# A fused attention and maxout kernel whose order table is planned anew with longer DMA steps

## The chip, the cores and the metric

The kernel runs on one core of a Trainium2 chip. The metric is device time in microseconds for one execution. Five engines work side by side, each through its own instructions in order: TensorE (PE in the profile; its weight loads are PEld), VectorE (DVE), ScalarE (ACT), GpSimd (POOL) and SyncE (SP), which here issues nearly all DMAs.

## The reference

Two layers follow each other. The first is attention with a threshold: only scores within `tau` of the row's maximum take part. The second is a feed-forward layer whose hidden value is the maximum of three products.

```
scores = q @ k.T / sqrt(64)                  # 8 batches, 8 heads, 576 rows
keep   = scores >= max(scores) - tau         # tau = 0.02
attn   = softmax(where(keep, scores, -1e9))
x      = attn @ v                            # laid out as 4608 x 512
h      = max(x @ w1, x @ w2, x @ w3)         # 4608 x 768
out    = h @ w_out                           # 4608 x 512
```

## The kernel before, in words

**The work.** A quad is four heads of one batch; there are 16. Its q and k are loaded (`qm`, `km`), transposed on PE (tile `tp`) and evacuated to `qt` and `kt`, by ACT or by DVE; POOL (in the first quad DVE too) makes `qs`, a copy of `qt` with its halves swapped. A quad has nine chunks of 128 rows by 2 x 576 scores, 144 in all; in batches 0 and 7 the nine are done in two parts, four and five.

**One half chunk** of 128 x 576 scores (tile `sc`, 288 of them) passes so: PE multiplies (letter `S`); DVE takes the row maximum (`m`), writing the negated scores to `z`; ACT makes the exponents in one or two passes (`e`, `n`); the sums lead to a reciprocal on DVE (`r`); POOL normalises into the bf16 tile `P` (`p`). A DMA transpose issued by SP turns a whole chunk (`t`, tile `ptq`); when a quad's chunks are there, PE multiplies them by v (`O` and `D`, tile `o`; a product), and the result is copied to `xt` (`x`, `w`).

**The feed-forward layer** follows batch by batch in pieces of two halves (`F` and `B`): hidden pieces (tile `ph`, from `xt` and the weights `w`), whose maximum is built by `h`, `H` and `v` in `hm` and `hT`, and output pieces (tile `po`), copied to `ob` by `u` or `U` and stored by `o`. The weights arrive in twelve loads (`g`) through borrowed tiles and are cast to bf16 by POOL, DVE or ACT (`z`, `b`, `f`).

**What sets the order.** `ORDER` is a text with one letter per step; the loop at the kernel's end walks through it, so the text fixes the order on every engine. A digit behind `S`, `T`, `F`, `N` or `O` names the PSUM bank, of which there are four, each large enough for one such tile. The case of some letters picks the engine: `A`, `c` evacuate on DVE, `a`, `C` on ACT; a threshold for the exponent is worked out on DVE by `s`, on POOL by `d`. `TILES` gives the order of the chunks within a quad's part. `MASKED` has one digit for each half chunk: 0 goes over `z`, with a threshold and two ACT passes; 1 has one ACT pass, and DVE removes what is below the threshold (`k`); 2 and 3 are as 0 and 1, but ACT reads the scores from PSUM directly, and 2 needs no threshold. In a direct half chunk the bank stays taken until ACT has read it.

The three tables were written by a planner that is not part of the file.

Of the kernel before, what the change touches and what calls it, by code (L numbers as in the profile page):

```python
# [35 lines left out]


# [10 lines left out]
ORDER = """
lllllllllllT1lT0lagqqcT3T2aS1CqqgS3mgS0emS2yynmeS1emgmT3eS0AeT2kgS3nqmT1CqAnT2rklS1eqmCS0nqmepS2eprrmS3emS1p
tmnS0pS3smnkpteeS2prmnzmtemepekpeS2lS0ylrbyS1nnlmtpnpmnrremptebS3peS0mnS1mS2znrpmS0eptmmnlpS3pemdlreekS0S1ms  # L50
kT3nAnO20lpeerwdDgpxtmnnT3S0eprectpmS2mtS3nprqS0mT1epAptT3S1plqenmbnO20CdrmpDlkxewzS3eegmlS0pF2mksBrF3HtS1Bd
S2nntqmeteepvlnF0BS1mqS3egvzRnppmT2nS0pmAndmrpS1peempeS2S1mgknpmegtretF3BkHS0tmS2pmetS1npS3mT2rsneF0zmsnyBcr
S1enpsvnO32S0peemDpwsmpwS1nF3S0smrzBrqS1nstmF2vBsT3S0ppemHenteAS1psF2mlT3zyBqrgcvsnS3F0nemgS2plpelnmepS3mtyB
ellqrmetqvnpS2sprdmO13fpsS0nDweS1mtewzkmnerS2S0F3dsnpS1mBpmeteepkF2mdtT0BnlulllneRnF1kAstS3pBHnmvF0epyRS2Btm
ppeS1S3vqtnmdS2F0pS1lpmneT3edCmpBF2emslnlT3aT1kHdqeBctRvS0ypF3S1ptnpmnmrdpBF2qS0S1vmenBmtedS3S0HepmnrqF1T2Bm
pseanS3velF2T0sT1CapkmBS0etvetS1rS3ppmmkmS0npnO21eetS3seDxrpmpnmqS0kytS3smpkxS2rmettpdS1emF0pesS3mmrS2nelBS1
nkmeqlduT3pmlpS2skeemCnO10kRsDwwldtS3pS1pmmtepeeF0S2qspdS3BmnmF1F2eneBBqhrkrF0S3pvpsBvT2S1snempndeapHterpllm
S3eF0mnS2dmS1myBqF3rF2nptS1vlsBsnBT0rmvpeS1ppnhncmS3mF2enntsrtF0BByevpF3rS1vemnppS2mF0eydBtS1thF2kBdBeS3tqmr
vevnlpO01S2DpnlmexkesemT2pwadF3eplS0kdT1tmBCqRHeS2dmpS0onS1nF3lmS2nmBelynnF0F1tpdtmqspBBevvphS3S2rS0nsseemF1
reF3ppmBntpBmrsdS0pveevS2nmmS1F3mlpertpT0BAypkepqS1UmnkF2tS0edS3entornS1mmBmtpeeueS3nS1ptkksrmmpO20ltnsrpDlk  # L60
S1rpS3mmxS2epxepT0mqcdnN1eT3AkdnBF2S0jS3meT1deBeqqcRF0S1pHBS2mtF3mBdnppS1monennpvdlrstS2vF0meeF3mBnherBkpevS
2lF1T0mappkslT3BrtvCnS2F0mpqS3S1detS2enBptmlmshpS3eS1prdmppmneF0lrlS2dF3ntBmmseBevsS2F1tpT0psBtrvymnAtS3hS2p
demnmO01S2kwenenpDS3ermT0nrwF2qlmtspncqpqrS1pedBF3mplevetS0plBS1mdeF2S0vpndBmmdorkhF3S1T2tBmS0eepS1ndatvdmtF
3pktndmRF2S0plemnpBdvBF1HS0mS3enpmrpnBeF2eT0CdqevBnlS3S1vepS0S2qptmmenmtkrsF3nS0edT1pmtlAemBT2srS1puqeS0pncm
nO32mekrtDweS0weqS1F2F3psmnpmnkplsS0eRkyepmByS1ekBmpsS0ypundmF2hS1RptemplBS0ndF3vdpmlT1BS2AdnmpevlF0S1BF2S3n
rlmBF1emdeehF0kpeBvnS3veemBsF2S1hrtS0ntplqBlnpF3mmnT1vBqsRtkyS0pF2tteCevS1omppBnS3S0hF2ptldpndmmBsenmS3pT1ye
aensvmeRS0etmpolS2skO31pDemT0wqwF2S3ctpdemBqF1ieS0T3pBvmS2tF0ndndaeF3hkymRdBqnvBF2pevsepS1lT0tBmpCrHpeS3ntS1
mS0nmdF2F3mBBS0perntnpevvpsnS1S2F3ltmrdepmepS0mBS2sT1kdmelUnF0tdS3nnpqmrS2ApnpT1BsemtS3RemnlN2CpS1kesBsppeer
qUlmeS0mmS3T1jT2tS0mdnasceltpO13menslqDypS0wknrxpS1mpmlyF3dT2BldS0eAspntHnnrS1pmtF2merpF3BqeBsS0vnenrvyF1S2B
enpS3mS0spptpmmmsS2heeF1rS3BpS0mF2nmF3mvteeBqtBF0eT1vHnkBF2S3dnsBrCnpF1vdemlS0BevqpykeF3mS2hrBprnmvF0eqtndts  # L70
S1prmleBO32nspDpvpeF1S0nwekS3wsBmnepdtS2hmF0T1mdpBS2AF3vS1erBF0etndmS2nmrnpeS1vBnF3mpsnT2ylpRpdCoeHmBpS0dS2e
vS1emmF3T0mBvS2asetpnnS0telpepqmmntrS1F3tpS2S0BmskeodmprtlknF1UeprmpqS2sT3eptcpmqsnBS0tS2mekudnS3O01Dkerpnmx
lexqrmpslS2dmpS3S1tF0mpleennermlS2BddF3mHnS1tpBrT0F2snmAS1eBevF0vpnptnqS3BmdlterHemtF2nslpS1tmBF0T3BpvsdCvyr
F1nedeS3rpltpeF2T0meBBS3tAHvmpF0F1qtqBpS2vnBS3pF0mS2mneBkerkhelO13tqnesmevsxklrpDS2nS1xF0T3pBmtmF1eCepkdS3S2
vBnrmpS0eS3phtmT2nF1mT0amnkpdBrqersvF3pS2BCF1S0mnT2BsevF3ompdrepqpS0thAmBdvS1peF2mtS0npBnmvS3S1S0deqrmpF2imT
3nBnptsreCpmqS3UmnseS0ekmtrodeF1petS2tmkepeBS3kO02psmtrDwN3ndpuexerpS0meF1S2BeF0mBBnjF2hnS1kyskvdeptBS0mmrF3
ptvdpS1nrpmBF0S2BnHnvF1epF3mBF0rveBBS2lykhF3vepS1mBnF0ddmS2F1venBS3mRtdHepmBnvS2depmS0oF3F1ptBmeBS0vehS3tnpn
knperlmsF2pF1mssBprvBppF3S0tvmeekBhnrteF2tS1F0BpmvsBenedS1nvmkrS3mpS2F0S1npetemrBmypeS2tO31umyspnDwwepO20xDe
skerpkS1pmF2S3oS1snrntextprpBpmnmF3F1BF0epUBnhprtBkdepF3F2ttvnprBtpBvhvF1pF3tBvBHoF0F2BBO13vDxvO20wDF3wwF1F2
F0oBHUuF1BBF2F3BhvoF0BvBiF1vF2BvF3BhvBvF2F1ouN0Bujooi  # L80
"""


# [728 lines left out]
```

## Time and profile before

| | |
|---|---|
| median of 3 runs | 441.38 us (440.68 to 441.64) |
| profiled execution, its own time | 440.52 us |
| its span | 438.7 us |
| PE busy | 418.6 us (95%) |
| DVE busy | 396.3 us (90%) |
| ACT busy | 393.7 us (90%) |
| POOL busy | 324.4 us (74%) |
| DMA transposes, median to landing | 144, 4.3 us |

The profiled execution lies 0.86 us under the median; sums are made against 440.52 us and carried over to the median. Every instruction of the kernel passes through one recording helper, so all rows of the profile name line 100, and groups are told apart by tile names (`z<-sc` writes `z` and reads `sc`). A PE matmul with fp32 operands stands as two matmuls in the profile. From step 72 on, two half chunks in eleven use the tile `stage` in place of `z`.

### The profile page before, as it was taken

How to read it: one execution, taken by the hardware profiler on the slowest of the kernel's cores; microseconds unless marked ns; L12 is line 12 of the kernel's file. 1: busy time of each engine (PE TensorE's matmuls, PEld its weight loads, DVE VectorE, ACT ScalarE, POOL GpSimd, SP SyncE). 2: the span in 40 equal slices, each digit the busy share in tenths (PEclk: the TensorE clock that was granted, in tenths of full speed). 3: DMA queues.
4: the chain of work that ended last, by engine and by line, in shares of the span. 5: the costliest groups of instructions: out<-in, count | busy, mean ns of one | idle time of the engine just before them, and what ended most of it. 6: DMA issues, size and time to landing. Idle time of an engine off the chain costs nothing.

```text
span 438.7 us, 14399 instructions
## 1 busy us (share of the span) xinstructions
PE 418.6 (95%) x5357; PEld 315.5 (72%) x5359; DVE 396.3 (90%) x1126; ACT 393.7 (90%) x813; POOL 324.4 (74%) x491
## 2 busy tenths in 40 slices
PE   8768889999999999999999999999999999999995
PEld 6455556775787877877787787877778777886962
DVE  3989999999999999999999999999999988998741
ACT  4999998999999999999999999999999999789412
POOL 3798999897689768878888868985887787467400
PEclk9969999999999999999999999999999999999999
DMA  9999999999998999999979997999998785788921
GB/s 264 317 232 228 205 265 249 246 202 224 232 199 177 261 211 226 164 234 201 211 157 213 267 220 153 167 233 191 233 198 156 182 192 83 155 149 155 206 87 73
DMA packets 211590, 87.98 MB, mean 201 GB/s; under 512 B 186944, under 2 KB 199744, under 8 KB 211520
## 3 DMA queue, kind: packets, MB, share of 16 engines
q1 hardware_dynamic: 210704, 86.40, 95.0%
q8 instruction: 42, 0.69, 0.7%
q10 hardware_dynamic: 816, 0.66, 0.5%
q14 instruction: 28, 0.23, 0.2%
HBM read 35.13 MB, written 9.44 MB: 102 GB/s over the span
## 4 chain that ended last, share of the span: by engine, by line
PE 76%; ACT 9%; DVE 6%; issue 3%; DMA 3%; POOL 1%; SPq 1%; DVEq 0%; POOLq 0%; ACTq 0%
PE ph L100 28%; PE sc L100 26%; PE po L100 10%; ACT z L100 8%; PE o L100 8%; PE tp L100 4%; DVE z L100 4%; DMA qm<-in_q_dram 2%; DMA ptq<-P 1%; DVE hm L100 1%; POOL P L100 1%; PE warm L100 1%; SPq L100 1%; DVE hT L100 0%; DVE kt L100 0%
## 5 line engine op out<-in xcount | busy, mean ns | idle before, releaser
L100 POOL TENSOR_SCALAR P<-z,rs 128x576 bf16<-128x576 f32 x250 | 193.3, 784 | 36.6 <-DVE rs L100 13.0
L100 DVE TENSOR_SCALAR_CACHE_REDUCE z<-sc 128x576 f32<-128x576 f32 x250 | 182.4, 750 | 9.9 <-PE sc L100 6.8
L100 PE MATMUL sc<-kt,qs 64*128 64x320 f32 (+2 forms) x640 | 181.5, 416 | 7.9 <-ACT z L100 5.0
L100 PE MATMUL sc<-kt,qt 64*128 64x256 f32 (+2 forms) x640 | 183.0, 427 | 0.9 <-ACT z L100 0.4
L100 PE MATMUL ph<-xt,w 64*128 64x288 bf16 (+2 forms) x2304 | 174.0, 283 | 0.4
L100 PEld LDWEIGHTS <-w 64*128 64x128 bf16 x2304 | 128.4, 94 | 30.8 <-issue 3.0
L100 ACT ACTIVATE z<-z 128x576 f32<-128x576 f32 x186 | 125.5, 679 | 0.3
L100 ACT ACTIVATE z<-z,th 128x576 f32<-128x576 f32 x159 | 118.6, 767 | 1.6 <-DVE th L100 1.0
L100 PEld LDWEIGHTS sc<-kt,qs 64*128 64x128 f32 (+1 forms) x640 | 91.9, 178 | 24.7 <-ACT z L100 7.4
L100 PEld LDWEIGHTS sc<-kt,qt 64*128 64x128 f32 (+1 forms) x640 | 91.6, 178 | 15.1 <-DVE z L100 2.5
L100 POOL COPY qs<-qt 64x640 f32<-64x640 f32 (+1 forms) x62 | 44.3, 715 | 15.9 <-ACT qt L100 9.1
L100 PE MATMUL po<-wo,hT 64*128 64x512 bf16 (+2 forms) x454 | 54.4, 354 | 0.8 <-DVE hm L100 0.4
L100 DVE SCALAR_TENSOR_TENSOR z<-z 128x576 f32<-128x576 f32 x64 | 51.5, 807 | 0.1
L100 POOL TENSOR_SCALAR th<-nm 128x1 f32<-128x1 f32 x95 | 28.6, 301 | 28.1 <-DVE z L100 11.9
L100 PE MATMUL o<-ptq,vb 128*64 128x512 bf16 (+4 forms) x720 | 43.5, 276 | 1.2 <-DMA ptq<-P 0.7
L100 ACT ACTIVATE z<-z,nm 128x576 f32<-128x576 f32 x57 | 43.1, 768 | 0.0
L100 PEld LDWEIGHTS <-hT 64*128 64x128 bf16 (+1 forms) x456 | 31.1, 94 | 15.7 <-issue 2.4
L100 DVE TENSOR_TENSOR hm<-ph,hm 128x576 bf16<-128x576 f32 (+2 forms) x48 | 36.1, 752 | 5.6 <-PE ph L100 4.5
L100 PEld LDWEIGHTS <-vb 128*64 128x64 bf16 (+1 forms) x720 | 26.0, 109 | 20.9 <-issue 10.4
L100 DVE TENSOR_TENSOR hT<-ph,hm 128x576 bf16<-128x576 f32 (+2 forms) x48 | 36.2, 753 | 2.2 <-PE ph L100 0.6
L100 ACT ACTIVATION_READ_ACCUMULATOR z<-z 128x1 f32 x186 | 36.7, 198 | 0.0
L100 POOL TENSOR_SCALAR P<-stage,rs 128x576 bf16<-128x576 f32 x38 | 29.0, 768 | 5.0 <-issue 3.1
(55 smaller groups left out, 413.8 us busy)
## 6 DMA issues: line engine op xcount, KB each, us to landing
vm<-in_v_dram SPq DMA_DIRECT2D x32, 256.0 KB, 3.9
qm<-in_q_dram SPq DMA_DIRECT2D x15, 512.0 KB, 4.7
km<-in_k_dram SPq DMA_DIRECT2D x15, 512.0 KB, 5.5
out_dram<-ob SPq DMA_DIRECT2D x14, 512.0 KB, 3.7
ptq<-P SPq DMA_TRANSPOSE x144, 4.3
v<-in_v_dram SPq DMA_DIRECT2D x16, 96.0 KB, 3.1
hT<-in_moe_w_dram SPq DMA_DIRECT2D x3, 512.0 KB, 10.0
stage<-in_moe_w_out_dram SPq DMA_DIRECT2D x3, 512.0 KB, 5.9
```

The costliest lines, as they stand in the source:

```text
L100: ins = fn(*a, **kw)
```

## The change

The planner was run anew with every step of the DMA queue counted four per cent longer. The file differs in the three tables alone: the order of steps, the digits of `MASKED`, the order of chunks in `TILES`, and the banks and engines that the letters name. The number of scores, products, hidden pieces, transposes and loads is what it was. Counted over the whole text, these letters change: `s` 94 to 85 and `d` 95 to 107; `r` and `R` together 128 to 131 instructions; `k` 72 to 73 and `n` 216 to 215; evacuations of `tp` on DVE 31 to 28 and on ACT 33 to 36; weight casts on DVE 3 to 5, on ACT 1 to 0, on POOL 8 to 7; output copies on DVE 7 to 6, on ACT 11 to 12. The direct digits among the first 72 half chunks go from 32 to 28.

```
 MASKED = """
-233222232202322222212300021210200220321222000000000310000010020100001001
+233222232222322222232320003102000200000001000000100310000010020100001001
...
 TILES = """
-065106157238447283620314785243875061513472860765830421817650432357816042
+106560512834787243321604785243871506351472608035786412817065432581376042
...
 ORDER = """
-lllllllllllT1lT0lagqqcT3T2aS1CqqgS3mgS0emS2yynmeS1emgmT3eS0AeT2kgS3nqmT1CqAnT2rklS1eqmCS0nqmepS2eprrmS3emS1p
+llllT2llT3ACqT2lqT3aS0lqqClS3meS1S2mmS0neelmeyS3mlymT1lAllS2keT1necT0rmqqnaggS3qlT1qnmS0CS1eeS2mpkrmpS3gepS0
...
```

At the very start the rows on PE are the same up to the first scores, but the tiles behind them are not: `T1 T0 T3 T2` took four banks for the first four groups of transposes, `T2 T3 T2 T3` takes two. PE before (`tp` with a number is one bank's tile; `qm`, `km` are the loads, `q9`, `k9` their ninth columns):

```order
L100 MATMUL tp_136<-identf_58,qm_116 128x64 x8
L100 MATMUL tp_136<-identf_58,q9_121 128x64 x2
L100 MATMUL tp_148<-identf_58,km_117 128x64 x8
L100 MATMUL tp_148<-identf_58,k9_122 128x64 x2
L100 MATMUL tp_169<-identf_58 128x128 x8
L100 MATMUL tp_169<-identf_58,qm_116 128x64 x8
L100 MATMUL tp_186<-identf_58 128x128
L100 MATMUL tp_186<-identf_58,km_117 128x64 x8
L100 MATMUL sc_197<-kt_167,qs_161 128x256
L100 MATMUL sc_197<-kt_167,qt_160 128x320
```

PE now:

```order
L100 MATMUL tp_126<-identf_58,qm_116 128x64 x8
L100 MATMUL tp_126<-identf_58,q9_121 128x64 x2
L100 MATMUL tp_139<-identf_58,km_117 128x64 x8
L100 MATMUL tp_139<-identf_58,k9_122 128x64 x2
L100 MATMUL tp_156<-identf_58 128x128 x8
L100 MATMUL tp_156<-identf_58,qm_116 128x64 x8
L100 MATMUL tp_175<-identf_58 128x128
L100 MATMUL tp_175<-identf_58,km_117 128x64 x8
L100 MATMUL sc_186<-kt_153,qt_150 128x256
L100 MATMUL sc_186<-kt_153,qs_151 128x320
```

`tp_156` lies in the bank of `tp_126`, so it waits for the evacuation of that tile. That evacuation has moved from ACT to DVE. DVE before, at the same place:

```order
L100 COPY qs_161<-qt_160 64x2x320
L100 COPY kt_167<-tp_148 128x2x320
L100 COPY qs_161<-qt_160 64x2x256
L100 TENSOR_SCALAR z_208,nm_209<-sc_197 128x576
L100 TENSOR_SCALAR z_216,nm_217<-sc_205 128x576
```

DVE now:

```order
L100 TENSOR_SCALAR qt_150<-tp_126 128x2x320
L100 COPY qs_151<-qt_150 64x2x320
L100 COPY qs_151<-qt_150 64x2x256
L100 TENSOR_SCALAR z_197,nm_198<-sc_186 128x576
L100 TENSOR_SCALAR z_207,nm_208<-sc_194 128x576
```

DVE evacuates `qt` first, and the copy to `kt` has gone to ACT.

The second place is POOL about two thirds through the program, where thresholds (`th`) have come over from DVE. POOL before:

```order
L100 TENSOR_SCALAR P_5664<-z_5406,rs_5659 128x576
L100 COPY qs_5522<-qt_5521 64x2x320
L100 CAST vb_5726<-vm_5273 128x1024
L100 TENSOR_SCALAR P_5751<-z_5464,rs_5659 128x576
L100 TENSOR_SCALAR P_5751<-z_5473,rs_5659 128x576
L100 TENSOR_SCALAR P_5765<-z_5476,rs_5723 128x576
L100 TENSOR_SCALAR P_5765<-z_5515,rs_5723 128x576
L100 TENSOR_SCALAR P_5809<-z_5558,rs_5723 128x576
```

POOL now, from the same normalisation (the 194th) on:

```order
L100 TENSOR_SCALAR P_5676<-z_5413,rs_5652 128x576
L100 TENSOR_SCALAR P_5690<-z_5456,rs_5652 128x576
L100 TENSOR_SCALAR th_5750<-nm_5629 128x1
L100 TENSOR_SCALAR th_5766<-nm_5684 128x1
L100 TENSOR_SCALAR P_5690<-z_5496,rs_5652 128x576
L100 TENSOR_SCALAR P_5785<-z_5530,rs_5779 128x576
L100 TENSOR_SCALAR th_5798<-nm_5707 128x1
L100 TENSOR_SCALAR P_5785<-z_5536,rs_5779 128x576
```

Three thresholds now stand between normalisations where none stood; each waits for a row maximum of DVE, and the normalisations behind it wait with it.

More of the change, by code (lines that the diff above doesn't have):

```diff
@@ L24 @@
 MASKED = """
-233222232202322222212300021210200220321222000000000310000010020100001001
+233222232222322222232320003102000200000001000000100310000010020100001001
 011010100100100000000010001100000000000111102100100000101000000100001100
-000000101000110100010000100001000100000100000100000100000001100010000000
-000011010010000000000001011100100000001110001100001001000110000012100010
+000000101000110100000100000001000100000100000100100100000000110000010000
+000011012010100000011001000000001000001110111000100010000110000012100010
 """
 TILES = """
-065106157238447283620314785243875061513472860765830421817650432357816042
-762315804786502134175623084406235781126835704862107435065150618732423748
+106560512834787243321604785243871506351472608035786412817065432581376042
+672305184652830714132860574471560328258061734720186435105616058732432748
 """
@@ L48 @@
 ORDER = """
-lllllllllllT1lT0lagqqcT3T2aS1CqqgS3mgS0emS2yynmeS1emgmT3eS0AeT2kgS3nqmT1CqAnT2rklS1eqmCS0nqmepS2eprrmS3emS1p
[L50 to L78, printed above, removed]
@@ L79 @@
-skerpkS1pmF2S3oS1snrntextprpBpmnmF3F1BF0epUBnhprtBkdepF3F2ttvnprBtpBvhvF1pF3tBvBHoF0F2BBO13vDxvO20wDF3wwF1F2
-F0oBHUuF1BBF2F3BhvoF0BvBiF1vF2BvF3BhvBvF2F1ouN0Bujooi
+llllT2llT3ACqT2lqT3aS0lqqClS3meS1S2mmS0neelmeyS3mlymT1lAllS2keT1necT0rmqqnaggS3qlT1qnmS0CS1eeS2mpkrmpS3gepS0
+lgmnnpmrkemerpS2pnetnS1pbpnmterS3mpreenkntmS2ppzS0mebernS1S3mmempS2eS0renpmmyenpttpllS1yemS3pmS2nllkS3T0derp
+mApsO21DrS0kneemwgrpgnT3nCwpT1S2mdptS3bqmteAzS2etlrmpmnnS1gpspemeS0ktT3S1dketmCO32DrenqS0tmnrtS1wdwF2ppppS3B
+nerqsmmmeenHS3brlnsnF1mlpqF0epdBevS2S3BnpnmgtstpmzS1eT2mrppS3ssrsvS1enpAmmS0netrepF2dmeS3ntBynmS1psF0lmsBgee
@@ new lines @@
+S3qpHS1nrngpvmO20kDsdgwtpT3qztmrwcpF2S1eBtS3nmeresS1pzvnF0yptsS2neBmmlF3mBnhS0ezT2geT1lbsravppmcS3S2eslnmqpe
+qlemS1nO23lrDkpF0mkdpxS2senwteRBpztmevS3nseS1S2S0msmF3tppS1msnemByeepkF2mdtT0BnlulkllneRnF1AnstS3pBHmvepyRF0
+S2BtmpeS1pvS3qmtnsS2F0pS1lpmneT3edCmpBF2emslnlT3aT1kHdqeBctpRvS0ypF3S1tnpmnmrdpBF2qS0S1vmenBmtdeS3HS0epmF1T2
+BnrqmpseanS3velF2T0sT1CapkmBS0etvpetS1rS3ppmmmkS0nnO21eeS3yDxS2prdemntpmS0pS3kmrqtskxmmtdS1eF2yS0epmmeendtpS
+3torkmBlS0nlpmT1selukdeS3kpenlCsO20DrS1emletwrS3qnppS2wtnpmF0eS1dBehqrpmdF3rnqmsF2tBmBkvsplF1ryspS0pvpeeBemH
@@ new lines @@
+lpT2S3S0epaS1F2mS3nnmmBqmnntrstesesrF0pvF1S3pnBBphT2tmtqdS3veneF0cS1neF2mBpmdntryBS1loF3vS0ppvmesmF2BS1nhekr
+sF0eBeBmnrvvpS3nO21S0klxmDT2mF3tpespetwasS0T1BdeklmRHS2qS0pmsClmtS1ypmppF3neS2nnpnsBF0mtF1qBeetnBsS2rhnvprpv
+S3smesS0F1F2dpmrmtBvelBevndlS0pneeS3mmeS1npF2T0BmprApnS3eF0kpeUmtS2nkqS1yrmemdpeS3tBeS1mS3kutnkrpesmmltnsO20
+xerppDkS1rplS3mpmxS2T0epN1mdqcneT3dABnkF2S0S3jomeT1decnBqRqF0eS1ptHBS2mdtF3mpBS1mlnepnpnvdrsvS2F0meeF3Bnlmhe
+rBS2pekvF1T0mkappslT3BtrvCnS2F0lmpS3S1qdeteS2nBptmtdhpmS3S1mpF0erdppemmnnlrldS2F3peBBmsespvF1S2tT0vrysmnpBhA
@@ new lines @@
+S3S2tdmetnmksrnO01eenpwS2DS3mptqT0eqnrewF2lmS1qcrenpptpdBF3mlepveS0plBmdoS1F2vS0ntBhdmdmF3S1ntreT2kBmS0epdS1
+lavdF3mnkptdmeRF2S0tpBdepmnpBvF1lHnS0mS3mprneeBpF2dT0CvBeS3vS1eS0S2nmpmmtqsneF3teS0rqdlkmlnpT1eAmBuT2rpcqS1p
+mpdeS0mtskneO23S1ierpS0ewklDmpkF2ednornemnteS1BtpqpwyS0muF3sS1mknBF2rorepryhdmS0pnBpeS1nF3mvmddT0BAS2dF1ypmS
+0BeF2vmnHtqnerS3BlF0pF1eedmrvBS3BpesvmF2lS0nnhktdlntppS3tdF1mlteBppBdmveS0T3nqvReCF2mS1mBpS3ntdhF0emS1pdrplT
+2BmS3teeadppeS1vmnlkmqS2snnpO30DrmqweT1F2xeytS0pcBS3mrpdvedF1T0mtBnnS2katF3epF0qHBndmlBS1rF2vdelvnmT3stBrylp
@@ new lines @@
+S0nepHCmelF1S3mS2eeF0pmsqBdpvpBS3nS2leS1ervnmpF0ytnsmS3BndpmkdS2rnmT3lrtprpUemenF1S0AesnetpppremS2T3mBkCN0Un
+dqS2yemBnqS1pnplrS3dS2mT1pjeaT0pmesmetrS3cO21eqkxpmDS0skS3ndxS2omdnepmeT1F0tRpF3BsApntqlmtyppS1BHmS2llvF0eF1
+mBnS3dvBS2ednnpetS0mrtmphF3dS1nS2mpernS0eBmqpmnvF1F2ddBeremtvppseBT0F3S1lCHknmBF2yddeF0eBpdvrvS1mBtF3eHtpS2t
+BmoF1envS0ptstBmslekneO32ynnkDqxvwF3S1eRnlBlmeS0S2HF1pndempT3mBptS0vsatdF2nS3BpqmnsF1S0RpyeBlmvedmS3HF2epT0n
+BS1etrspCperS0mevpqtpmS3nF2mdT1aetBS0pmnpeS1qS3vF2nmrmpS1eemBlkntdmpS0krptmkS3F1nndT0meRllpBenpS3UsmqtS2CS0u
@@ new lines @@
+mpmeO31tpedpeDnS0rktokxdxenprtS2S1eF3mdS0empmdsBtmF2erS1T0BHpmF3epS1lnBvnnAnF2epS0vlpsBllmmF3S1rBF0hmyvnpree
+T2CBtF1pS3dT2kBvmkttersppasF0S3mtF2hlBBvpeS1nF3vnyeemdS0rF2pBlmS1BhqdknpO03msvoertlwneeS1mDrwdepnS2qT1nF0qnp
+F3BncS1BmvS2dppherpS0mprpmS3dF1pT2BnpadmqeeqetmnsT0F3svS2BcF1S0nmT2vBatmkrsF3pdeheS0qrqtnmenBtS2eF1vmS0tpymB
+eS3S2vpeS0eF1rmT3npdpBmqmcS3pS0F2etuettkeS1mmmnS3kBrO01pDuexN2S0kkpnrmxkmdRsF3dF1BBpjhlBpS2okF3vS0mmF1edneBB
+nS0eveF2S3BHtpesmpmvntprF1eS0dtmF3BpBS2nhpF0vF3mkBdpvBrpS1ennrmeF2dvpS0eBrtmdF1sS3tpneBS0mhvS2mnF3F1tBmeikve
@@ L81 @@
+BpF2heeS0pnS3F1spmremBBvdtnrtpF3S0BevmhS1F2pppknF3BmrvBndS1sevtnmkrdS0mpS2eF3eS1BnpemretmypS2tO01upysmnDwwee
+pO23xDskerkS1pnmS0F2oS1srnewtrBptpmnpmF0F1F3epUtBBnphrkBdeppF0F2ttvnprtpBvhBF1pF0vtBvBhoF3F2BBO10vDxvO23wDF0
+wwF1F2F3oBHUuF1BBoF2F0BhvF3BvBiF1vF2BvF0BHvBvF2F1ouN3Bujooi
 """
```

## The prediction

> **What bounds the kernel now.** I read three views in this order: the busy times by stage, the chain that ended last, the list of waits. Stages first (columns: PE busy and instructions in brackets, PEld, DVE, ACT, POOL, granted PE clock, DMA share, GB/s):
>
> ```profile
> 20.00:26.00 6.00, 2.31 (x16) 1.31 (x15) 5.41 (x16) 6.00 (x14) 6.00 (x7) 1.00 1.23 187
> 26.00:33.00 7.00, 6.32 (x29) 5.05 (x27) 6.05 (x17) 7.00 (x18) 7.00 (x10) 0.51 1.13 250
> 60.00:100.00 40.00, 37.56 (x501) 27.69 (x503) 38.72 (x117) 38.52 (x81) 36.03 (x53) 1.00 1.09 234
> 100.00:400.00 300.00, 298.76 (x3942) 231.49 (x3939) 287.08 (x826) 288.91 (x594) 231.23 (x362) 1.00 0.98 195
> 400.00:439.00 39.00, 33.93 (x486) 23.85 (x482) 19.70 (x43) 14.15 (x29) 9.32 (x13) 1.00 0.53 122
> ```
>
> Until about 100 us ACT leaves nothing idle (6.00 of 6, 7.00 of 7) and PE waits. From 100 to 400 us PE is idle for 1.24 us in 300, while ACT has 11.1 us to spare. After 400 us PE finishes the feed-forward layer alone. So the end is set by how early PE becomes the only limit, and then by PE's work, whose pieces the change leaves alone. The chain that ended last (start, duration, what) says where the handover lies:
>
> ```profile
> 20.20 8.65 ACT z L100 x19
> ...
> 103.45 3.76 ACT z L100 x8
> ...
> 111.83 5.05 DMA ptq<-P
> 117.13 2.66 PE o L100 x37
> ...
> 122.41 2.95 PE ph L100 x48
> ```
>
> ACT's exponents carry it until 111 us, then one transpose, and at 117.13 us the second product of batch 1 (the sixth of 20; I call it product 5, counting from 0) passes it to PE, which keeps it. Of the waits, these matter below (total, times, longest):
>
> ```profile
> PE sc L100 <- ACT z L100: 5.3, 7, 3.0
> PE tp L100 <- DMA qm<-in_q_dram: 0.7, 1, 0.7
> PE o L100 <- DMA ptq<-P: 0.7, 1, 0.7
> ```
>
> PE waited once for a transpose, 0.7 us, at product 5, and once for a load. A planner that counts DMAs longer can win back no more than that there; the rest of its new order has to earn or lose elsewhere.
>
> **The change part by part.** *The start.* The first steps of the profiled execution (start, duration):
>
> ```profile
> 5.19 0.37 PE L100 MATMUL tp<-identf,q 64*128 64x64 f32 x2
> 5.59 0.70 ACT L100 ACTIVATE qt<-tp 128x640 f32<-128x640 f32 x1 [2.04 <-PE tp L100]
> 5.84 1.09 PE L100 MATMUL tp<-identf 128*128 128x128 f32 x8
> 6.44 0.95 POOL L100 COPY qs<-qt 64x640 f32<-64x640 f32 x1 [5.16 <-ACT qt L100]
> 7.82 0.45 PE L100 MATMUL sc<-kt,qs 64*128 64x256 f32 x1
> 8.67 0.76 DVE L100 TENSOR_SCALAR_CACHE_REDUCE z<-sc 128x576 f32<-128x576 f32 x1 [0.24 <-PE sc L100]
> ```
>
> Before, PE's filler transposes began at 5.84 us in a fresh bank. Now they reuse the bank of the first `qt` and wait for its evacuation, which has moved to DVE, where it costs 819 ns for ACT's 696 to 699 (rows below): 5.59 + 0.82 is 6.41, and with the 0.04 to 0.06 us by which a successor follows here, 6.45. That is 0.61 later than 5.84, and filler, transposes and first scores stand behind it in PE's order, so scores begin at 8.43 and the first maximum at 9.28. The other operands don't come later: POOL's `qs` would end at 6.44 + 0.12 + 0.95 = 7.51, and `kt`, now on ACT, before that. The lag is worth 0 if ACT's idle time takes it up later (1.48 us from 60 to 100), 0.61 if not. I take +0.6, because the chain runs through ACT without a break from 10 to 29 us.
>
> *Engine choices.* The rows for what moved (busy us, mean ns):
>
> ```profile
> L100 DVE SCALAR_TENSOR_TENSOR z<-z 128x576 f32<-128x576 f32 x64 | 51.5, 807 | 0.1
> L100 ACT ACTIVATION_READ_ACCUMULATOR z<-z 128x1 f32 x186 | 36.7, 198 | 0.0
> L100 ACT ACTIVATE z<-z 128x576 f32<-128x576 f32 x186 | 125.5, 679 | 0.3
> L100 POOL TENSOR_SCALAR th<-nm 128x1 f32<-128x1 f32 x95 | 28.6, 301 | 28.1 <-DVE z L100 11.9 <-DVE stage L100 7.0 <-DVE rs L100 2.7
> L100 DVE RECIPROCAL rs<-sm 128x2 f32<-128x2 f32 x112 | 17.1, 157 | 1.6 <-ACT z L100 1.2
> L100 DVE TENSOR_SCALAR th<-nm 128x1 f32<-128x1 f32 x94 | 13.2, 144 | 0.1
> L100 DVE COPY ob<-po 128x1024 f32<-128x1024 f32 x6 | 7.3, 1218 | 0.9 <-PE po L100 0.9
> L100 ACT ACTIVATE ob<-po 128x1024 f32<-128x1024 f32 x8 | 8.1, 1013 | 0.9 <-PE po L100 0.8
> L100 ACT ACTIVATE kt<-tp 128x640 f32<-128x640 f32 x10 | 7.0, 699 | 1.1 <-PE tp L100 1.0
> L100 DVE TENSOR_SCALAR qt<-tp 128x640 f32<-128x640 f32 x8 | 6.6, 819 | 0.1
> ```
>
> Over the whole program ACT gains three evacuations (at most 3 x 0.70 = 2.1 us) and an output copy (1.0), loses a cast (as many elements as that copy, so about 1.0) and one second exponent pass with its accumulator read (0.88): +1.2. DVE gains a masked pass (0.81), three reciprocals (0.47) and two casts (an estimate of 1.7 from evacuations of 640 at 0.82, scaled down to less than the 1.22 of a 1024-element fp32 copy), loses nine thresholds (1.30), three evacuations (at most 2.46) and an output copy (1.22): -2.0. POOL gains twelve thresholds (3.6) and loses a cast (about 1.0): +2.6. What matters is only the part ahead of the handover, since behind it ACT has 11.1 us idle, DVE 12.9 and POOL 68.8 to cover it; were that cover gone, the whole +1.2 of ACT would show. Counting letters up to the tenth feed-forward piece, where both texts have issued 60 half chunks of scores, 16 groups of transposes and 4 products, ACT has two evacuations and a hidden copy more and a cast and an `xt` copy less, some +0.2 us, and DVE four thresholds and two casts more and two evacuations and a hidden copy less, some +0.7. The end is moved by between 0 and 0.7; I take +0.2, ACT's, since ACT carries the chain there.
>
> *Product 5.* In letters, the last normalisation stands 58 ahead of the product, formerly 49, and no load has come between its transposes on SP. The wait of 0.69 us can go, or stay because the chunk is itself late by the start's lag: -0.7 to 0, and I take -0.3.
>
> *The other products.* How tight the others were (issue of the last transpose on SP, then the product; landing times of all transposes, shortest, median, longest):
>
> ```profile
> 159.65 1.27 SPq L100 DMA_TRANSPOSE ptq<-P  x1
> 164.20 1.16 PE L100 MATMUL o<-ptq,vb 64*64 64x512 bf16 x14
> 361.11 1.27 SPq L100 DMA_TRANSPOSE ptq<-P  x1
> 364.41 1.81 PE L100 MATMUL o<-ptq,vb 64*64 64x512 bf16 x26
> DMA to landing us min/median/max: 3.2/4.3/7.4
> ```
>
> Product 7 began 4.55 us after its last transpose was issued, 1.3 us more than the shortest landing; product 15 began 3.30 after, 0.1 more. In the new text PE has six pieces between the last normalisation and product 7 (eight before) and five ahead of product 15 (three before), each of about 0.49 us (half a hidden piece is 8 matmuls, and 48 take 2.95 us in the chain). So 7 loses about 1.0 of its margin and keeps 0.3, 15 gains 1.0. Cost 0, with 0 to +1 for 7.
>
> *The rest.* SP's first loads and weights change places with transposes; the fourth transpose now has no load ahead of it, and the first weights are needed only after two products. I cost that at 0: PE's only DMA waits of any size were the two in the list. The last 60 letters are the same but for banks, one store and one copy: 0. Sum: 0.6 + 0.2 - 0.3 = +0.5, or 441.0 us against the profiled 440.52; against the median, which is 0.86 higher, 441.9.
>
> **The rivals.** *Faster: the half clock does not come.* PE's longest wait for ACT, and what DVE waited for after it:
>
> ```profile
> 24.99 0.53 PE L100 MATMUL sc<-kt,qs 64*128 64x320 f32 x1 [3.04 <-ACT z L100]
> 25.94 0.76 DVE L100 TENSOR_SCALAR_CACHE_REDUCE z<-sc 128x576 f32<-128x576 f32 x1 [0.37 <-PE sc L100]
> 30.48 0.76 DVE L100 TENSOR_SCALAR_CACHE_REDUCE z<-sc 128x576 f32<-128x576 f32 x1 [0.64 <-PE sc L100]
> 32.40 0.76 DVE L100 TENSOR_SCALAR_CACHE_REDUCE z<-sc 128x576 f32<-128x576 f32 x1 [0.31 <-PE sc L100]
> ```
>
> PE stood idle for 3.04 us because its banks were held for ACT, and behind it the granted clock was 0.51 for 7 us, in which DVE waited three times for scores, 1.32 us. Four direct digits fewer among the first 72 hold banks less long. If the idle stretch falls apart, these 1.32 us go, and with product 5's whole wait (0.4 more than I took) the time is 441.9 - 1.7 = 440.2. Against it: ACT was fully busy all through the stretch, so PE must idle as much, and only its spread can change; and the chain crosses PE there only at its end. The Trainium skill, "TensorE: Matmul & The Clock Gate", Part 1, says that the clock is halved after an idle window of about 3.4 us and restored after a busy one. The trace agrees in kind (3.04 us idle, then 0.51). By that rule alone, with a phase that nobody sets, the stretch may come and go between executions of one kernel, and the gain would not belong to the change.
>
> *Slower: a threshold on POOL holds up a product.* POOL works in order; a threshold placed early waits for its maximum, with normalisations behind it. The waits from 100 to 400 us:
>
> ```profile
> POOL th L100 <- DVE z L100: 11.4, 10, 2.9
> ```
>
> The longest was 2.9 us. There are twelve more, ten of them between the products 9 and 15. One such wait ahead of a product with 0.1 to 0.3 us of margin puts up to 2.8 us of idle time on PE, which has nothing to make it good after 117 us: 441.9 + 2.8 = 444.7, and about 447 if it happens twice. It decides as soon as POOL is later by more than the margin. For it: the margins, and that ten such waits fell into this stage already. Against it: from 100 to 400 us POOL is idle a quarter of the time.
>
> *No change at all: the start's lag is taken up* by ACT's idle time ahead of product 5, and the engine choices cancel: 441.4.
>
> **How the numbers follow.** A measurement of this kernel tells 0.2% from no change, 0.9 us: faster is below 440.5, slower above 442.3. My sum +0.5 has chance 0.40, with its own range 440.9 to 443.0 from the bounds (0 to 0.6, 0 to 0.7, -0.7 to 0, 0 to +1), rather above 442.3 than not since small misplacements on a PE without slack add and seldom subtract: of the 0.40, 0.11 is within and 0.25 above, 0.04 below. POOL's threshold 0.28, all slower. No change 0.10, 0.07 of it within. The half clock or an earlier handover 0.22, of which 0.20 is faster and 0.02 within. Faster 0.26, same 0.20, slower 0.54. The range reaches from the faster rival, less 0.7 for a start without its lag, to nearly the doubled threshold: 439.5 to 446.5.
>
> **What would show it.** Right: the first maximum near 9.3 us; product 5 near 117 us without a wait for its transpose; PE idle from 100 to 400 us by 1 to 2 us; 33 to 34 us busy after 400. Wrong: a granted clock of 1.00 throughout; a first maximum at 8.7; any PE wait over 1 us after 117 us, most of all a product waiting for `ptq` with a POOL threshold behind its lateness.

## The result and the profile after

| | before | after |
|---|---|---|
| median | 441.31 us (440.68 to 441.64) | 445.85 us (444.66 to 449.06) |
| ratio | | 1.0118, 95% interval 1.0087 to 1.0149 |
| profiled execution, its span | 440.52 us, 438.7 us | 449.06 us, 447.3 us |

The kernel became 1.2% slower: +4.5 us by the medians, where I had forecast +0.5. The profiled execution of after is the longest of its four; the others took 444.66 to 446.35 us. A second profile of the unchanged file, called "after again" below, has a span of 443.3 us.

The stages of after, in the columns shown before:

```profile
26.00:33.00 7.00, 4.47 (x24) 2.29 (x24) 7.00 (x20) 6.42 (x14) 6.96 (x9) 0.92 0.97 170
60.00:100.00 40.00, 34.94 (x462) 25.30 (x464) 36.15 (x107) 37.41 (x79) 33.33 (x47) 1.00 1.14 215
100.00:400.00 300.00, 297.53 (x3896) 226.52 (x3892) 284.06 (x806) 287.58 (x589) 233.42 (x372) 1.00 0.97 196
```

Between 60 and 100 us every engine did less: PE 34.94 us for 37.56 before, DVE 36.15 for 38.72, POOL 33.33 for 36.03. When all of them fall together, what they wait for may lie outside them. The chain that ended last names two loads:

```profile
59.38 7.53 ACT z L100 x17
66.94 4.13 ACT z L100 x9
73.06 1.91 POOL P L100 x2
78.98 8.15 DMA q<-in_q_dram
92.23 1.45 POOL P L100 x2
101.21 4.82 DMA qm<-in_q_dram
...
123.30 2.53 PE o L100 x36
```

Behind 20 us two loads stand on it, of 8.15 and 4.82 us. Before's chain had one there, the fourth quad's q, and none behind it:

```profile
45.52 6.90 DMA qm<-in_q_dram
```

Product 5 begins at 122.64 us instead of 117.13 (the row at 123.30 is what is left of it behind a pause). The waits, PE's and then one of POOL's:

```profile
PE sc L100 <- ACT z L100: 6.1, 5, 1.8
PE tp L100 <- DMA qm<-in_q_dram: 3.0, 3, 1.7
PE tp L100 <- DMA q<-in_q_dram: 1.1, 2, 0.8
PE tp L100 <- DMA km<-in_k_dram: 1.0, 1, 1.0
```

```profile
POOL P L100 <- DMA ptq<-P: 7.2, 3, 4.6
```

PE waits 5.1 us for loads of q and k, against 0.7 before. POOL waits 7.2 us (2.3 before) for transposes to free the `P` tiles they read, once for 4.57 us, up to 89.78 us.

To see where time is lost over the whole run I used a clock of work. All the kernels have the same 5,357 matmuls. I weighted each by its columns and passes (halved where it uses 64 rows) and took from each trace the moment at which a given share of that sum has started. The table shows how far each run lies behind the profiled execution of before, in us:

| share of PE's work (time in before) | 10% (65.7) | 20% (110.7) | 30% (151.4) | 60% (272.9) | 75% (333.4) | 85% (372.4) | 99% (428.8) |
|---|---|---|---|---|---|---|---|
| after | 2.5 | 6.3 | 6.8 | 6.7 | 7.3 | 8.5 | 8.7 |
| after again (e4) | 1.5 | 2.4 | 2.6 | 2.7 | 3.3 | 4.5 | 4.7 |
| changed first part (e1) | 1.7 | 3.1 | 2.8 | 2.1 | 1.9 | 1.9 | 1.9 |
| changed second part (e2) | 1.0 | 1.4 | 1.4 | 1.4 | 2.0 | 3.2 | 3.5 |
| one load late (e6) | 7.3 | 6.6 | 6.3 | 6.3 | 6.3 | 6.3 | 6.3 |
| engine letters only (e7) | 0.3 | 0.7 | 0.8 | 2.1 | 5.3 | 10.8 | 10.8 |
| order only (e8) | 0.6 | 0.1 | 0.7 | 2.9 | 5.7 | 15.6 | 17.2 |
| burst broken (e13) | 0.0 | 1.2 | 1.3 | 1.3 | 1.8 | 3.1 | 3.3 |

There are two losses, one ahead of about 110 us and one behind 60% of the work, some 273 us. From 30% to 60% the two profiles of after keep their delay within 0.1 us.

### The profile page after: what moved, and what is told of

Same layout as the page of the kernel before. It is cut to its first block, busy times and chain, and to the rows that moved or that the text cites. A ratio compares the mean times of both kernels' runs of the same rounds, so it can differ in the third digit from the quotient of the medians.

```text
span 447.3 us, 14400 instructions
## 1 busy us (share of the span) xinstructions
PE 421.2 (94%) x5357; PEld 311.7 (70%) x5359; DVE 398.2 (89%) x1120; ACT 397.0 (89%) x814; POOL 327.2 (73%) x502
## 4 chain that ended last, share of the span: by engine, by line
PE 76%; ACT 8%; DVE 6%; DMA 4%; issue 2%; POOL 2%; SPq 1%; DVEq 0%; POOLq 0%
PE ph L100 28%; PE sc L100 27%; PE po L100 9%; PE o L100 8%; ACT z L100 8%; DVE z L100 4%; PE tp L100 3%; DMA q<-in_q_dram 3%; POOL P L100 1%; DMA qm<-in_q_dram 1%; SPq L100 1%; POOL qs L100 1%; DVE w L100 0%; DVE hm L100 0%; DVE hT L100 0%
## 5 line engine op out<-in xcount | busy, mean ns | idle before, releaser
L100 PE MATMUL sc<-kt,qs 64*128 64x256 f32 (+2 forms) x640 | 181.1, 416 | 7.7 <-ACT z L100 3.6
L100 PE MATMUL sc<-kt,qt 64*128 64x320 f32 (+2 forms) x640 | 183.5, 427 | 4.0 <-ACT z L100 2.5
L100 ACT ACTIVATE z<-z,th 128x576 f32<-128x576 f32 x165 | 123.0, 767 | 5.4 <-POOL th L100 2.8
L100 PEld LDWEIGHTS sc<-kt,qs 64*128 64x128 f32 (+1 forms) x640 | 89.3, 177 | 27.2 <-ACT z L100 7.7
L100 PEld LDWEIGHTS sc<-kt,qt 64*128 64x128 f32 (+1 forms) x640 | 89.5, 177 | 18.5 <-ACT z L100 5.0
L100 POOL TENSOR_SCALAR th<-nm 128x1 f32<-128x1 f32 x107 | 32.5, 304 | 24.4 <-DVE z L100 7.1
L100 PE MATMUL o<-ptq,vb 128*64 128x512 bf16 (+4 forms) x720 | 45.7, 276 | 1.6 <-DVE hm L100 0.5
L100 ACT ACTIVATE z<-z,nm 128x576 f32<-128x576 f32 x55 | 41.4, 767 | 0.0
L100 PEld LDWEIGHTS <-hT 64*128 64x128 bf16 (+1 forms) x456 | 29.7, 94 | 16.1 <-issue 1.8
```

Source lines behind the costliest of these rows:

```text
L100: ins = fn(*a, **kw)
```

## The experiments

**Where is it lost: e1 to e4.** At step 511 of the old text and 516 of the new one the two kernels are in the same state (61 half chunks begun, the same banks taken, the same masks in flight), so the texts can be cut there and crossed, and the other two tables with them. The numbers count steps, not characters.

```diff
 e1:  ORDER = changed[:516] + before[511:]     # first part new
 e2:  ORDER = before[:511] + changed[516:]     # second part new
 e3 (changed kernel):
-... T2 l q T3 ...      +... T1 l q T2 ...     # third and fourth T in fresh banks
 e4:  the changed kernel, unchanged
```

> The three tables of the new kernel up to the eleventh feed-forward piece (61 half chunks issued, about 88 us into the profiled run), and those of the kernel before from there on; both texts stand in the same state there, with the same tiles in the same banks, so nothing else is changed. Theory A, the time is lost in the first 88 us: +4.5 us against before, 445.9. Rival B, it is lost behind that point, by POOL's thresholds or by products that come too early: about 441.4 plus the start's 0.6, 442.

> The reverse: the kernel before up to the same state, the new tables from there on. Theory A: 441.4, no more than 0.5 us from before. Rival B: +3 to +4.5 us, 444.4 to 445.9, with new PE waits after 120 us.

> The new kernel with two digits changed: the third and fourth group of transposes of the first quad go to the banks 1 and 2, so that the filler transposes need not wait for DVE's evacuation. Theory A with the start's lag as one part of the loss: the first maximum moves from 9.62 to 8.7 to 8.9 us and the time falls by 0.6 to 0.9 us, to about 445.1. Rival, the lag is taken up by later idle time: less than 0.2 us. Rival, the lag is what all later lateness comes from: 3 us or more are won.

> The new kernel unchanged, for a second profile. Its profiled execution of 449.06 us was the longest of four. Theory A: 445.9 us in the median, and the profile again shows PE waiting for loads (q, k) between 50 and 110 us, for 2 to 5 us in all, and POOL waiting for transposes near 85 us, where before shows 0.7 and nothing. If those waits are chance, they are gone and the loss sits elsewhere.

Before ran at 440.47 us on this chip. Measured: e1 442.61 (ratio 1.0045, 1.0022 to 1.0067), e2 444.05 (1.0075, 1.0052 to 1.0099), e3 446.56 (1.0132, 1.0102 to 1.0161), e4 445.63 (1.0116, 1.0088 to 1.0144). Neither theory alone is right: the first part costs 0.45%, the second 0.75%, and together they make the whole 1.16%. The table of delays says where in the second part: 2.1 us of it (1.4 to 3.5) lie behind 60% of the work. The other 1.4 us of e2's profile had formed by 110.7 us, 1.0 of it by 65.7, where its text is still that of before; a load of q had landed late at its start (below). So the 3.6 us of the medians are not all shown to be the second part's. In e1 the load waits are there again: PE stood for 2.14 us until 56.66 us, ahead of its transposes of the fourth quad's q, which landed at 56.52; the list of waits puts this down to DVE. No gain from the start showed: e3 has its first maximum back at 8.65 us and is not faster than e4, though the two intervals leave room for 0.6 us.

**The loads of the first part: e5 and e6.** Moving the fourth quad's q is the smallest test of the load waits. e5 issues it earlier in the changed kernel (the load in front of it has to come along), e6 issues it later in the kernel before, behind three transposes.

```diff
 e5 (changed kernel)
-k e t m C ... b r l n s n F1 m l p
+k l l e t m C ... b r n s n F1 m p
 e6 (kernel before)
-e g m l S0 ... n n t q m e t e e
+e g m S0 ... n n t q m e t l e e
```

> The changed kernel, with two loads issued about 45 steps earlier: the second half of the third quad's ninth v rows and, right behind it, the fourth quad's q (qm), both now ahead of the eighth to eleventh of the transposes behind which the changed text issues them. Nothing else moves. Theory L (late loads): TensorE waited 1.7 us for this qm at 56.9 us in the changed kernel run again, and 0.7 us before; issued at about 46 us and landed by 53 us it isn't waited for. The wait falls below 0.5 us and the time goes from 445.6 to 444.0 to 444.8. Rival D (elementwise engines): DVE, ACT and POOL are 91 to 98% busy between 30 and 75 us and set the pace there, so that a wait of TensorE is repaid within some us: 445.3 to 446.0, with the wait gone.

> The mirror image: the kernel before, with the fourth quad's qm issued behind three more transposes than it was, as the changed kernel has it; nothing else moves. Theory L: the wait of TensorE for qm at 52.6 us grows from 0.7 to 2 us or more, and the time from 440.5 to 441.5 to 442.5, which would be half or more of the 2.1 us that the changed first part cost. Rival D: the wait grows just as much and the time stays at 440.4 to 441.0.

e6: 445.82 us against 440.18 (ratio 1.0120, 1.0101 to 1.0140), for one load moved by 22 letters. PE's wait and the stages around it:

```profile
PE tp L100 <- DMA qm<-in_q_dram: 5.6, 2, 5.4
```

```profile
53.00:57.00 4.00, 0.35 (x4) 0.00 (x0) 1.55 (x6) 3.54 (x9) 3.83 (x7) 1.00 0.87 168
57.00:64.00 7.00, 5.25 (x31) 3.91 (x33) 3.67 (x9) 2.33 (x5) 1.51 (x3) 0.51 1.19 367
```

PE stood for 5.4 us, the granted clock was 0.51 from 57 to 64 us, and DVE, ACT and POOL, which I had called the pace makers, emptied out behind it (3.67, 2.33 and 1.51 us of 7). The delay stood at 6.3 us, to 0.1, from 30% of the work to the end. Rival D is out: a wait of this size here is paid in full. The size was larger than expected because the load, once moved, queued behind transposes that themselves waited for POOL. It also went one transpose further than the changed kernel has it: SP issues this q behind 10 transposes in before, behind 12 in after and behind 13 in e6. So e6 shows what such a place can cost, not what this one cost in after.

e5 gave the opposite sign of what I expected: 448.02 us (1.0182, 1.0165 to 1.0198), slower than after itself. The wait for q is gone, but the three transposes that q passed (three by SP's rows, the tenth to the twelfth) became later, and with them the load of k behind them:

```profile
PE tp L100 <- DMA km<-in_k_dram: 3.9, 1, 3.9
```

**Is the queue itself the limit: e9 and e13.** SP's DMA issues (with what they wait for) take 62.0 of the 66 us from 20 to 86 us in before, and 60.5 in after. The Trainium skill, "Perfetto Trace Analysis", Optimizing DMA Performance, names an issuing engine whose track is solid with DMA slices as a limit of its own, the slices being descriptor generation. The trace agrees on the solid track (94 and 92%), not on what fills it, and no run here tried a second queue. SP's own list of waits, in before from 20 to 90 us, puts 38.4 us down to POOL, most of it to one row:

```profile
SPq L100 <- POOL P L100: 31.8, 18, 3.8
```

So SP's track is full to a good part because a transpose stands in it until POOL has made its `P`. And a full track by itself need not cost anything: in after it is 94% taken from 240 to 280 us as well, where the delay does not grow. If the queue is the limit, putting both loads early (e9) only moves the wait, while taking a transpose that can't go yet out of the loads' way (e13) helps.

```diff
 e9 (changed kernel): as e5, and k's load from behind the 16th transpose (as counted from 1) to ahead of the 13th
-n p n m g t s t p ...          +n p n m g l t s t p ...
 e13 (changed kernel): the 20th transpose behind four of the loads
-F0 y p t s S2 ... e s l n      +F0 y p s S2 ... e s l t n
```

> The changed kernel with both loads of the fourth quad earlier: its q as in the run with the loads early, and its k (km) too, ahead of the twelfth to fifteenth transposes instead of behind them. That run had lost the wait for qm and got one of 3.9 us for km at 69 us, and was 2.4 us slower than the changed kernel. Theory L (the load that TensorE reaches first has to be landed; nothing else matters): no wait for a load above 0.5 us before 75 us, and 443.2 to 444.8. Theory Q (SP's queue is full from 20 to 85 us, so whatever is issued ahead of the transposes makes them late, and the same time is lost at the next thing that is waited for: a transposed P, or a q or v further on): 445 to 448.5.

> The changed kernel with its 20th transpose, which waits on SP for POOL ahead of six loads (three v and w_out, qm, km and q), moved behind the first loads of that group, where the kernel before has it. Theory Q (SP's queue is full, and the order in it decides who waits): in the profiled execution of the changed kernel the transpose behind those loads took 5.5 us to issue and POOL then waited 4.6 us for a free P; in another execution of the same kernel it took 4.1 us and POOL waited for nothing there, and that one was 4 us shorter. With the loads spread, POOL's wait stays under 1 us, the runs lie closer together (within 1.5 us) and the median is 444.3 to 445.2 against 445.6 to 445.9. Rival B (the burst is a symptom, the lateness is from the loads at 57 and 66 us): 445.4 to 446.2 and as much scatter as before.

e9: 447.49 us (1.0119, 1.0083 to 1.0154), in two groups, 443.95 and 444.02, and 447.24 to 448.73: nothing won. Its profiled execution, one of the long ones, has no load wait ahead of 75 us, and then q 0.93 us at 87.58 and POOL 4.1 us at 90.24 for its `P` tiles.

e13: 444.01 us (443.67 to 445.15; 1.0083, 1.0067 to 1.0100), some 1.5 us less than the changed kernel by the ratios, and no run above 445.2. This is the one edit of the changed kernel whose time fell. The interval just overlaps those of after and of e4, so the size is uncertain. What the edit does is seen in the rows. After, SP's issues and then POOL (start, duration):

```profile
75.78 0.67 SPq L100 DMA_DIRECT2D vm<-in_v_dram  x1
76.56 0.53 SPq L100 DMA_DIRECT2D stage<-in_moe_w_out_dram  x1
77.14 0.64 SPq L100 DMA_DIRECT2D vm<-in_v_dram  x1
...
78.98 0.47 SPq L100 DMA_DIRECT2D q<-in_q_dram  x1
79.49 11.49 SPq L100 DMA_TRANSPOSE ptq<-P  x4
89.78 1.46 POOL L100 TENSOR_SCALAR P<-z,rs 128x576 bf16<-128x576 f32 x2 [4.57 <-DMA ptq<-P]
```

Burst broken:

```profile
71.47 0.66 SPq L100 DMA_DIRECT2D vm<-in_v_dram  x1
...
74.65 2.52 SPq L100 DMA_TRANSPOSE ptq<-P  x1
77.22 0.58 SPq L100 DMA_DIRECT2D km<-in_k_dram  x1
77.85 0.47 SPq L100 DMA_DIRECT2D q<-in_q_dram  x1
78.36 8.11 SPq L100 DMA_TRANSPOSE ptq<-P  x4
```

In after six loads are issued from 75.78 us on, since the transpose ahead of them waited for POOL; the four transposes behind them take 11.49 us to issue (the first alone 5.5), and POOL runs out of `P` tiles. With the burst split the first load goes 4.3 us earlier, the four transposes take 8.11 us, and POOL's wait of 4.57 is gone. After again stands between them: its first load goes at 74.31 us, the four transposes take 9.95, and POOL is not starved there. So the burst leaves it to small shifts whether POOL runs dry, which fits the scatter of the changed kernel. But some 2.5 of the 4.3 us are not the edit's: at 65.7 us, ahead of it, this execution was already that much ahead of after's (0.0 and 2.5 in the table). From 10% to 20% of the work e13 loses 1.2 us, with one wait for `qm` of 1.5 us until 101 us; after loses 3.8 there, and after again, with the burst whole, 0.9. So where the 1.5 us of the medians come from is not shown.

**Load and consumer: e12 and e14.** In the kernel before, q is waited for 0.7 us, and a weight load stands right ahead of it. e12 exchanges the two; e14 also moves POOL's cast of that weight behind three normalisations.

```diff
 e12 (kernel before)
-e e g m l S0          +e e l m g S0
 e14: also
-v z R n p p m T2 n S0 p m      +v R n p p m T2 n S0 p z m
```

> The kernel before with two neighbours on SP's queue exchanged: the fourth quad's q (qm, issued at 45.5 us, landed at 52.4, waited for 0.7 us) goes ahead of the weight load in front of it, which costs the weight half a microsecond. Theory L: the wait of 0.7 us falls to 0.1 or less and the time to 439.6 to 440.1, against 440.2 before. Theory D (the elementwise engines repay such a wait): 440.2.

> The kernel before with the fourth quad's q ahead of its neighbour, a weight load, as in an earlier run, and POOL's cast of that weight moved behind the three normalisations that followed it. In the earlier run the weight landed at 52.5 instead of 49.3 us, POOL stood 2.2 us in front of the cast, DVE and TensorE behind it, and TensorE then ran at half clock for 7 us. Theory Q: with the cast behind, neither q nor the weight is waited for; no half clock after 40 us; 439.3 to 440.2 against 440.2 to 441.3 for the kernel before. Rival: the hidden pieces at 56 us need the weight, and wait for the later cast instead: 441 or more.

e12: 441.28 us, from 439.09 to 444.78 (1.0014, 0.9989 to 1.0039); e14: 440.21 (1.0000, 0.9988 to 1.0011). Neither beats the kernel before, so no version beats both. But e12's profile is the clearest example of what a place in SP's queue is worth. Its rows, in order of time:

```profile
52.62 1.04 POOL L100 CAST w<-ob 128x1024 bf16<-128x1024 f32 x1 [2.20 <-DMA ob<-in_moe_w_dram]
54.42 0.76 DVE L100 TENSOR_SCALAR_CACHE_REDUCE z<-sc 128x576 f32<-128x576 f32 x1 [2.08 <-POOL P L100]
56.06 0.51 PE L100 MATMUL sc<-kt,qs 64*128 64x320 f32 x1 [2.82 <-DVE qt L100]
56.16 0.78 ACT L100 ACTIVATE z<-z,th 128x576 f32<-128x576 f32 x1 [2.53 <-POOL th L100]
```

The weight landed 3.2 us later (52.5 for 49.3), and four engines stood for it in turn: POOL before its cast, DVE for a buffer that POOL's next step frees, PE for a tile that DVE evacuates, ACT for a threshold behind the cast. In before that cast began at 50.49 us without a wait. In e14 the cast begins at 52.44 us, waits for nothing, and neither does PE for q; the range of 5.7 us shrinks to 2.3. The gain of 0.7 that theory Q gave was not measured.

**The second part: order or engines: e7, e8, e10, e11.** These leave the order of steps and exchange engine letters behind step 511.

```diff
 e7  (before): s>d 30, d>s 22; h>H 5, H>h 4, w>x 4, x>w 3, A>a 3, C>c 3, c>C 1, U>u 1
 e8  (second part of the changed text): the same letters back, d>s 30, s>d 22, H>h 5 ...
 e10 (before): only s>d 30, d>s 22
 e11 (before): only the 24 others
```

> The kernel before in its own order, with the engine letters of the changed kernel from step 511 on: 52 thresholds change places between DVE and POOL (30 to POOL, 22 to DVE), and 24 evacuations and copies between DVE and ACT. Masks, tile order, banks and the order of steps stay. Theory P (POOL's thresholds, the slower rival of the prediction): the loss behind the 61st half chunk, 3.6 us in the run of the changed second part, is in the engine choices: 442.5 to 444.0. Theory O (order): the same scores, products and copies in another order, each waiting a few tenths for a bank or a tile, with the engine choices worth under 0.6 us: 440.3 to 441.2.

> The complement: the kernel before up to step 511 and the changed text behind it, as in the run of the changed second part, but with the engine letters of the kernel before for thresholds, evacuations, product copies, output copies and hidden copies. Theory O: the loss stays, 443.2 to 444.8. Theory P: it goes, 440.3 to 441.5. If the order and the engine choices fit only each other, both this run and the one with the engine letters alone are slower than before by more than 2 us.

> The kernel before with only the 52 thresholds behind step 511 put on the engine that the changed kernel has for them (30 from DVE to POOL, 22 from POOL to DVE). With all engine letters of the changed kernel it was 10.8 us slower. Theory P (POOL's thresholds hold up its normalisations): 444 to 451, most of the 10.8 us. Theory E (the copies: an evacuation on an engine that is busy at that moment keeps a bank taken, and TensorE's next score waits for it): 440.2 to 442.

> The complement of the run with the thresholds only: the kernel before with only the 24 evacuations and copies behind step 511 on the engines of the changed kernel. Theory E: 445 to 451. Theory P: 440.2 to 442. If the two add up, the two excesses together make about 10.8 us.

e7: 451.02 us (1.0248, 1.0233 to 1.0263). e8: 457.90 (1.0403, 1.0383 to 1.0423). e10: 443.62 (1.0056, 1.0039 to 1.0073). e11: 448.81 (1.0178, 1.0158 to 1.0197). Order and engine letters fit only each other: each alone is far slower than the two together (444.05), the third outcome named in advance. Of e7's 10.8 us the thresholds make 2.6 and the copies 7.8, which add up to 10.5. So the larger part is the copies', as theory E has it. That an evacuation on an engine that is busy at that moment keeps a bank taken, the waits show in part. From 270 to 400 us the list of PE's waits is empty in before, and in e11 it begins with an evacuation and a product copy on ACT:

```profile
PE ph L100 <- ACT qt L100: 0.9, 1, 0.9
PE ph L100 <- ACT xt L100: 0.7, 1, 0.7
```

In e8 the waits name more of it. Before has no row like the first and the last, and 1.3 and 0.7 us in the other two:

```profile
PE sc L100 <- ACT kt L100: 4.1, 3, 2.6
PE sc L100 <- DVE z L100: 3.0, 6, 0.9
PE sc L100 <- DVE kt L100: 1.7, 3, 1.0
PE sc L100 <- DVE qt L100: 1.5, 2, 0.8
```

Even so the list of waits shows only part of it. In after, the list has 0.7 us of waits of PE behind 118 us, and from 30% of the work (151 us) on the table of delays shows 1.9 us lost. By the profile's legend a matmul's end is modelled, so a wait shorter than a matmul can stay inside a busy row.

**A short wait, taken away: e15.** In e2 two such places can be read off: the product at 367 us, whose last transpose landed at 367.47 us, and the product at 343 us, whose halves the new text parts by a score.

```diff
 e15 (e2)
-B m q m c S3 p S0                          +B m p q m c S3 S0
-... l w n e e S1 m D r w                   +... l w n e e D S1 m r w
```

> The kernel before up to step 511 and the changed text behind it (444.0), with two steps moved by one or two places: POOL's last normalisation for the product at 367 us goes ahead of a q swap of 1.1 us, and the second half of the product at 343 us ahead of the score that the changed order puts between its halves. Theory W (behind 275 us the loss of 2 us is a sum of short waits of TensorE, 0.2 to 0.5 us each): the product waits less than 0.1 us for its transposed P instead of 0.5, and 0.5 to 0.8 us are won: 443.2 to 443.6. Rival G (each short wait removed is replaced by the next): 443.9 to 444.8.

Measured: 443.12 us (1.0050, 1.0030 to 1.0069), against 1.0075 for e2; the intervals overlap, so the times alone decide nothing. The traces do. The product before, in e2 and in e15:

```profile
364.41 2.58 PE L100 MATMUL o<-ptq,vb 64*64 64x512 bf16 x40
```

```profile
367.11 3.02 PE L100 MATMUL o<-ptq,vb 64*64 64x512 bf16 x40
```

```profile
369.13 2.54 PE L100 MATMUL o<-ptq,vb 64*64 64x512 bf16 x40
```

The 0.48 us by which the middle row is longer than the last are the wait, and there all of it is won: across this product e2 falls behind by 0.4 us and e15 by 0.0. By the clock of work some 0.35 us of it are left at the end. The reason for the wait stands on POOL. Before, e2, e15:

```profile
359.34 0.60 POOL L100 COPY qs<-qt 64x512 f32<-64x512 f32 x1
360.03 0.22 POOL L100 TENSOR_SCALAR th<-nm 128x1 f32<-128x1 f32 x1
360.34 0.74 POOL L100 TENSOR_SCALAR P<-z,rs 128x576 bf16<-128x576 f32 x1
```

```profile
362.24 1.13 POOL L100 COPY qs<-qt 64x512 f32<-64x512 f32 x1
363.46 0.75 POOL L100 TENSOR_SCALAR P<-z,rs 128x576 bf16<-128x576 f32 x1
```

```profile
363.43 2.04 POOL L100 TENSOR_SCALAR P<-z,rs 128x576 bf16<-128x576 f32 x2
365.53 0.60 POOL L100 COPY qs<-qt 64x512 f32<-64x512 f32 x1
```

In e2 the swap for the next quad, twice as long as usual, goes ahead of the last normalisation, which ends at 364.21 us; the product begins 2.9 us later. The other repair did the reverse: the halves of the product at 343 us now touch, and a transpose behind them waits 0.5 us for DVE, so that about a quarter of a microsecond more is lost there than in e2. One place followed theory W, the other rival G.

## Why the prediction was wrong

The direction was right. The time lay inside the range of 439.5 to 446.5 us by luck: the upper end stood on POOL's thresholds holding up two products, which no trace shows. The size was off by 4.0 us, and two steps of the sum carry it.

**"The rest", costed at 0, is the first loss** (2.0 to 2.6 us: e1, and after again at 30%). I argued that "PE's only DMA waits of any size were the two in the list". That told how well the old order had placed its loads, not that their places were free. SP's queue is over 90% taken from 20 to 86 us, and a load that changed places with transposes there was late for its reader (after, e1, e6) or made another late (e5). e6 prices one such exchange, a larger one than the change makes, at 5.6 us, and e13, with one transpose moved, is some 1.5 us faster. No edit took the whole loss away, so the cause is shown as to its kind, not counted out wait by wait. How much of the first part's loss comes from its engine choices and masks (my +0.2) was not separated and stays open; so does what puts an execution of e9 into one group or the other.

**"Behind it ACT has 11.1 us idle, DVE 12.9 and POOL 68.8 to cover it" is the second** (2.0 to 2.1 us in the profiles). The idle sums hardly differ after (from 100 to 400 us ACT 12.4, DVE 15.9, POOL 66.6, from the rows above), and PE lost time all the same. Where PE had no slack, a sum of idle time covered nothing: what counts is whether this bank or that tile is free at the moment at which PE reaches it. e10 and e11 move 2.6 and 7.8 us with the same steps in the same order, only some of them on another engine. Only the 0.4 us at one product are shown place by place; the other 1.6 us are located (behind 273 us) but not traced to single steps.

The other points. *The start*: the lag came as described. PE's filler waits for DVE, and the first maximum is at 9.62 us, in after again at 9.21, for 9.28 forecast:

```profile
5.97 0.82 DVE L100 TENSOR_SCALAR qt<-tp 128x640 f32<-128x640 f32 x1 [5.97 <-PE tp L100]
6.86 1.09 PE L100 MATMUL tp<-identf 128*128 128x128 f32 x8 [0.57 <-DVE qt L100]
9.62 0.76 DVE L100 TENSOR_SCALAR_CACHE_REDUCE z<-sc 128x576 f32<-128x576 f32 x1 [0.18 <-PE sc L100]
```

What it is worth at the end stays open: e3 took it away and won nothing that can be measured. But e2, which has the start of before, began its first maximum at 9.57 us because a load of q landed late (PE waited 0.96 us), and it was still 1.0 us behind at 65.7 us. So the start moves by as much by itself, and a lag of that size was not taken up there. *Product 5* did not lose its wait for the transpose; the wait moved inside the product, where the list puts it down to nothing ("issue"):

```profile
122.64 0.40 PE L100 MATMUL o<-ptq,vb 64*64 64x512 bf16 x2
123.30 2.53 PE L100 MATMUL o<-ptq,vb 64*64 64x512 bf16 x38 [0.25 <-issue]
```

The second row begins 0.09 us after the transpose issued at 117.96 us had landed (123.21); in after again it is 119.56 and 119.47. Before, the third matmul followed the first after 0.12 us, here after 0.66, so some 0.5 us of the 0.69 stayed. And the product came 5.5 us later, so the term of -0.3 had nothing to stand on. *Product 7* waited for nothing (0, as forecast). *Product 15* went the wrong way: I gave it 1.0 us more margin by counting PE's pieces between its last normalisation and its start, and it lost 0.4. The count left out POOL's own order, where the swap of 1.13 us had come ahead of that normalisation; I had counted the steps on PE, not those on the queue that the late step sits in. *PE idle from 100 to 400 us*: 2.47 us for 1 to 2 forecast; 1.7 of it is one wait for a load of q, near 105 us, since the handover had moved into the window. After 400 us PE was busy 42.6 us for 33 to 34 forecast, since its work lay 8.7 us later. No wait of PE above 1 us came after 117 us, as forecast.

*The rivals.* The half clock did shrink, from 6.8 us to 3.4 (31.8 to 35.2 us, granted 0.92 over 26 to 33), and nothing that lasted was gained: by the clock of work after is 0.15 us ahead at 30 us of before's time and 1.7 behind at 36. DVE and ACT set the pace there (7.00 and 6.42 of 7). The rival's condition came true without its price. POOL's thresholds were the wrong culprit: they waited 7.1 us for maxima in `z` in after, less than before (11.9), 16.9 for 22.1 with all their waits, and product 15, which waited, had a swap ahead of it. Moved alone they do cost 2.6 us (e10), so the mechanism exists, but the change had placed the rest of its order to suit.

## What to carry to other kernels

Before costing a reordering, look at the issuing queue as an engine of its own: sum its issue rows by stage, and where it is over 90% taken and its readers have no time to spare, follow each load that changes places to its reader and each step it passes to theirs. In a stage where the bound engine has no slack, idle sums of the others were no cover here; look at the moment at which each bank or tile comes free, on the queue of the step that frees it. And a table of orders and engine choices that was made as one piece cannot be judged by halves: here the new engine choices alone cost three times, and the new order alone five times, what both cost together.
